# Attention that mixes into token rows, with gate columns, in a fused attention and expert kernel

## The chip, the cores and the metric

One core of a Trainium2 chip. The metric is the device time of one execution in microseconds; runs of one kernel agree within some 0.2%.

## The reference

Two stages run one after the other. The first is a linear attention with a complex decay, for 4 batches, 8 heads, 768 time steps and 48 features a head:

```
mag   = sqrt(a_re^2 + a_im^2);  scale = min(mag, 0.999) / (mag + 1e-6)
S     = (a * scale)[t] * S + k[t] v[t]^T        # S complex, 48 x 48 a head
y[t]  = q[t] . Re(S)
```

Its output, 3072 tokens of 384 features, goes to a mixture of 8 experts. Gate logits are `x @ w_gate`; tokens are assigned greedily by descending logit with a capacity of 384 tokens an expert; each expert computes `relu(x @ w1) @ w2` for its tokens. All data is fp32.

## The kernel before

The 3072 tokens are cut into 24 tiles of 128 (function `unit(i)`); six tiles are one batch. Three tiles form a group (`GC = 3`, 8 groups), on which the elementwise work runs in 1152 columns (`elementwise`). Groups 0 and 7 are cut in two pieces.

*Elementwise.* The decay is turned into running sums of logarithms and angles along time, so that a tile's recurrence becomes matrix products. Stages F1 and F2 square `ar` and `ai` on ScalarE (ACT) into the tiles `s1` and `s2`; F6 adds the two squares. For the groups in `BY_DMA` (groups 1 to 6) F6 is a DMA of GpSimd's queue (POOL) that accumulates `s1` into `s2` (in the trace s<-s); for the others it is an addition on VectorE (DVE). F7 to F10 take logarithm and exponential, S is the scan over time, G3 and G5 scale queries and keys (kq<-kq,s and kq<-kq,zi), N0 scans the angles, T1 and T3 make sines and cosines (tile `CS`). ACT loads one table for exponentials and another for angles in turn; `PLAN` says which stages share a table.

*Per tile.* RK and RQ rotate keys and queries by `CS` into a buffer `f` of 768 columns (f<-kq,CS; `F_BUFS = 4` buffers). Stage K copies `f` into the head-major tile `KQ` with 8 DMAs of SyncE's queue (SP), one a head. Then PE computes the scores (SC, tile sc), DVE masks them (MK, am<-sc,mask), PE transposes the keys (FL, tile kp), ACT copies them out (KC, tile KT), PE multiplies keys by values (ST, tile U) and adds the old state (CA, U<-W,ident), and DVE multiplies by the decay into the next state `W` (WM, W<-U,KQ). The last tile of a batch has no state step, its first one no carry.

*The output of a tile.* MX writes y with features as rows and tokens as columns: the weights are 64 columns of V or W (48 of the head and 16 that belong to the next), the streamed operand is 128 columns of masked scores or queries. A matrix product in fp32 shows as two instructions. ACT copies y out (XC, tile xT). FN turns xT back into token rows by a product with `pick`, a matrix that holds an identity and the gate weights: 96 feature columns and 8 logit columns for each of 4 head pairs (tile xp). ACT copies the features to x and, for the first 18 tiles, the logits to LP (XE); DVE sums the logits over the head pairs (LR, logits<-LP or logits<-xp); a DMA stores x to the token array xd in HBM (XS). The values are loaded in token rows (`load_v`), two groups deep.

*Order.* Every step is recorded with an engine, a cost, a priority and its dependencies (`op`). The planner `in_order` then simulates the engines with these costs, a hop between engines (`HOP`) and a step on one engine (`STEP`), and emits the instructions in the order that it finds; each engine executes its queue in that order. A step's priority is its tile number plus an offset of its kind from the table `OFF`. Where the planner sees PE idle, it puts in filler products (tile hot). The engines' instructions are chained, so nothing reorders them later.

*After attention* the routing finds each expert's tokens, and `experts` gathers token rows from xd, multiplies, and scatters the results. Its order comes from the same planner with its own constants (those whose names begin with M_).

Of the kernel before, what the change touches and what calls it, by code (L numbers as in the profile page):

```python
# [25 lines left out]
GC = 3  # L26
# [30 lines left out]
def constants(nc, con, z, w_gate):  # L57
    v, g = nc.vector, nc.gpsimd

    def t(n, shape, dt=F32):  # L60
        x = con.tile(shape, dt, name=n)
        setattr(z, n, x)
        return x

    jp = t("jp", [128, 128], I32)
    g.iota(jp, pattern=[[1, 128]], base=0, channel_multiplier=-1)
    v.tensor_scalar(t("ident", [128, 128]), jp, 0.0, None, op0=OP.is_equal)
    v.tensor_scalar(t("mask", [128, 128]), jp, 0.0, None, op0=OP.is_ge)
# [12 lines left out]
    t("pid", [128, 1])  # L81
    pick = t("pick", [128, 4, 104])
    v.memset(pick, 0.0)
    for s in range(2):
        r = slice(64 * s, 64 * s + 48)
        v.tensor_copy(pick[r, :, 48 * s:48 * s + 48], z.ident[r, None, r].to_broadcast([48, 4, 48]))
        g.dma_start(pick[r, :, 96:104], w_gate[:, s].rearrange("p d e -> d p e"))
# [157 lines left out]
def attention(nc, real, tc, z, q, k, a_re, a_im, v_tok, xd, later):  # L245
# [8 lines left out]
    LP = con.tile([128, 6, 4, 8], F32, name="LP")  # L254
    v, g = nc.vector, nc.gpsimd
    for i in range(2):
        w = con.tile([96, 400], F32, name=f"W{i}")
        g.memset(w, 0.0)
        W.append(w)
# [5 lines left out]
    for i in range(2):  # L265
        x = con.tile([128, GC, 432], F32, name=f"V{i}")
        g.memset(x[:, :, 384:], 0.0)
        VT.append(x)
# [20 lines left out]
    def dve(n):  # L289
        return n / 960 + 0.1  # L290

    def scan_(n):
        return n * 2.15 / 960 + 0.06

    def dve2(n):
        return n / 1920 + 0.11

    def sca(n, bias=False):
        return n / 1200 + (0.23 if bias else 0.14)
# [46 lines left out]
    def load_v(gi):  # L346
        b, c0, n = GROUPS[gi]
        r = b * S + c0 * 128
# [125 lines left out]
    def unit(i):  # L474
# [3 lines left out]
        v_ = VT[gi % 2]  # L478
# [4 lines left out]
        def KQ():  # L483
            return tiles["KQ", i]

        for hh in range(2):
# [11 lines left out]
            op(("MK", i, hh), "dve", 0.64, at, mask, [("SC", i, hh), ("MX", i - 2)])  # L498
        if cc < 5:
            for hh in range(2):  # L500
# [9 lines left out]
                op(("KC", i, hh), "act", 0.44, at, copy, [("FL", i, hh), ("ST", i - 2), ("ST", i - 3)])  # L510

            def state():
                U = ps.tile([128, 384], F32, name="U")
                mine["U"] = U[:96]
                for h in range(8):
                    for r in HALVES:
                        nc.tensor.matmul(U[r, h * 48:h * 48 + 48], KT[i % 2][:, h * 96 + r.start:h * 96 + r.stop],
                                         v_[:, c, h * 48:h * 48 + 48], start=(h == 0), stop=(h == 7 and not cc), skip_group_check=True)

            def carry():  # L520
                nc.tensor.matmul(mine["U"], z.ident[:96, :96], W[cc % 2][:, :384], start=False, stop=True,
                                 skip_group_check=True)
            op(("ST", i), "pe", 1.33, at - 0.2, state, [("KC", i, 0), ("KC", i, 1), ("lv", gi), ("WM", i - 1), ("WM", i - 2)])
            if cc:
                op(("CA", i), "pe", 0.65, at - 0.1, carry, [("ST", i), ("WM", i - 1), ("WM", i - 2)])
            else:
                made["CA", i] = made["ST", i]

            def gate():
                return KQ()[:, :, 256:257].to_broadcast([96, 8, 48])  # L530

            def nxt():
                return W[(cc + 1) % 2][:, :384].rearrange("p (a b) -> p a b", a=8)
            op(("WM", i), "dve", 0.52, at,
# [3 lines left out]
        def mix():  # L538
            Wc = W[cc % 2]
            y = ps.tile([128, 4, 128], F32, name="y")  # L540
            mine["y"] = y
            for p in range(4):
                for inter in range(2 if cc else 1):
                    for h in (2 * p, 2 * p + 1):
                        o = y[64 * (h % 2):64 * (h % 2) + 64, p]
                        e = slice(h * 48, h * 48 + 64)
                        if inter:
                            nc.tensor.matmul(o, Wc[:, e], KQ()[:, h, 128:256], start=False, stop=True)
                        else:
                            nc.tensor.matmul(o, v_[:, c, e], mine["am", h // 4][:, h % 4], start=True, stop=(cc == 0))  # L550

        def evac():
            xT = wk.tile([128, 4, 128], F32, name="xT")
            mine["xT"] = xT
            nc.scalar.activation(xT, mine["y"], AF.Copy)

        def turn():
            xp = ps.tile([128, 4, 128], F32, name="xp")
            mine["xp"] = xp
            for p in range(4):  # L560
                for r in HALVES:
                    nc.tensor.matmul(xp[r, p, :104], mine["xT"][:112, p, r], z.pick[:112, p], start=True, stop=True)

        def out():
            x = wk.tile([128, 4, 96], F32, name="x")
# [8 lines left out]
        def logits():  # L574
            if i >= MOST:
                v.tensor_reduce(z.lg[:, i], mine["xp"][:, :, 96:104].rearrange("p a e -> p e a"), op=OP.add, axis=AX.X)
# [7 lines left out]
        op(("MX", i), "pe", 1.9 if cc else 1.0, at, mix,  # L584
           [("MK", i, 0), ("MK", i, 1), ("lv", gi), ("XC", i - 1)] + ([("WM", i - 1)] if cc else []))
        op(("XC", i), "act", 0.54, at - 0.1, evac, [("MX", i), ("FN", i - 2)])
        op(("FN", i), "pe", 0.9, at + 0.6, turn, [("XC", i), ("XE", i - 1), ("LR", i - 1)])
        if i == nu - 1:
            op(("LR", i), "dve", 0.45, at, logits, [("FN", i)])
        op(("XE", i), "act", 0.46, at, out, [("FN", i), ("XS", i - 2)] + ([("LR", i)] if i == nu - 1 else []))  # L590
        op(("XS", i), "dma", 0.546, at, store, [("XE", i)])
        if i < nu - 1:
            op(("LR", i), "dve", 0.15 if i % 6 < 5 else 0.45, at, logits, [("FN", i)])
# [4 lines left out]
    for gi in range(G):  # L598
# [10 lines left out]
        if gi + 2 < G:  # L609
            load(("lv", gi + 2), 2.2, elementwise_at + 4, load_v(gi + 2),  # L610
                 [("MX", gi * GC + c) for c in range(GC)] + [("ST", gi * GC + c) for c in range(GC)])
    for n, fn in enumerate(later):
        op(("later", n), "dve", 1.0, NT - 1.0, lambda fn=fn: fn(nc), [("later", n - 1)])
# [45 lines left out]
BY_DMA = [(gi, 0) for gi in range(1, 7)]  # L659
# [4 lines left out]
OFF = {"A1": 7.7532, "F1": -8.0, "F10": -0.2852, "F11": 6.1629, "F2": 1.0958, "F3": 3.1048, "F4": 3.0098, "F5": -8.0, "F6": 8.0, "F7": -6.5322, "F8": 3.2365, "F9": 5.0508, "FL": 2.946, "FL<": -3.9259, "FN": 4.3835, "G1": -0.6071, "G2": 4.4992, "G3": 8.0, "G4": -8.0, "G5": -5.9505, "K": 1.9006, "KC": -0.4768, "LR": -3.8173, "MK": -2.5243, "MX": -4.6482, "N0": 0.976, "N1": -8.0, "N2": -5.5169, "P0": -6.2872, "R0": -7.514, "R1": -4.516, "R2": 3.2639, "R3": 4.827, "R4": -4.8476, "R5": -0.5791, "S": 6.954, "SC": 3.4101, "SC<": -8.0, "ST": 0.3675, "ST<": -0.421, "T1": 7.9956, "T2": 6.9667, "T3": -8.0, "TL": 5.7027, "UA": -3.4084, "UA<": -5.1223, "WM": 0.1274, "XC": 7.799, "XC<": -7.3842, "XE": 4.4086, "XS": 0.7846, "la": -5.6357, "later": -8.0, "li": -5.3368, "lk": -1.3428, "lv": 6.2134, "RK": -2.7051, "RQ": -3.6666, "table": -0.5748, "CA": 3.7656, "BE": -7.9653}  # L664
CHAIN = ("scalar", "vector", "tensor", "gpsimd", "sync")
F_BUFS, KC_BUFS = 4, 5
# [767 lines left out]
def _lay_out(inputs):  # L1434
    import numpy as np

    def feature_major(a):
# [9 lines left out]
        "v": c(inputs["v"].transpose(0, 2, 1, 3)).reshape(N, DM),  # L1447
# [19 lines left out]
```

## Time and profile before

| | us |
|---|---|
| median of 3 timed runs | 517.16 (516.69 to 517.54) |
| the profiled execution | 518.87 |
| its span, first to last instruction | 517.1 |
| PE, DVE, ACT, POOL busy in the span | 433.3, 408.0, 273.5, 93.3 |
| DMA queue of SP: share of 16 engines' span | 27.5% |
| DMA queue of POOL: share | 24.2% |

Engines are PE (TensorE; PEld is its weight load), DVE (VectorE), ACT (ScalarE), POOL (GpSimd) and SP (SyncE, which here only issues DMAs). In a row of instructions, out<-in names the tiles; an "idle" time with an arrow names what ended the wait.

### The profile page before, as it was taken

The numbers are of one execution on the slowest core, as the hardware profiler recorded it, in microseconds if no ns is written. First come the engines' busy times: TensorE is split into PE (matmuls) and PEld (weight loads), VectorE is DVE, ScalarE is ACT, GpSimd is POOL, SyncE is SP. The second block draws the span as 40 slices with busy tenths as digits, with TensorE's granted clock in tenths as the row PEclk, the third lists the DMA queues.
The fourth block names the chain that finished last, engine by engine and source line by source line (L and its number), as shares of the span: only waits on it lengthen the run. The fifth ranks groups of instructions, "written<-read, shape, count | busy, mean of one in ns | idle before, by whom it ended". The sixth has DMA issues, their size and how long they took to land.

```text
span 517.1 us, 10712 instructions
## 1 busy us (share of the span) xinstructions
PE 433.3 (84%) x4138; PEld 377.7 (73%) x4147; DVE 408.0 (79%) x1182; ACT 273.5 (53%) x436; POOL 93.3 (18%) x127
## 2 busy tenths in 40 slices
PE   0008889798989998995699999999999999999992
PEld 0007768585868787895588679888988789999991
DVE  6989879998899999745846699798998998755420
ACT  6996868896878795711012444254424525354410
POOL 3000101010010000000020422425222242530101
PEclk9999999999999999997599999999999999999997
DMA  7866878898888676631260623562160623660101
GB/s 241 252 187 160 232 206 274 222 229 268 236 250 255 189 237 185 190 104 47 67 225 1 225 112 136 185 259 78 36 270 31 260 77 138 253 251 5 43 0 46
DMA packets 47234, 86.11 MB, mean 167 GB/s; under 512 B 5344, under 2 KB 41056, under 8 KB 45136
## 3 DMA queue, kind: packets, MB, share of 16 engines
q1 hardware_dynamic: 39104, 42.56, 27.5%
q0 software_dynamic: 7648, 42.29, 24.2%
q8 instruction: 32, 0.52, 0.4%
q10 hardware_dynamic: 432, 0.59, 0.3%
q14 instruction: 18, 0.15, 0.1%
HBM read 53.49 MB, written 9.44 MB: 122 GB/s over the span
## 4 chain that ended last, share of the span: by engine, by line
PE 32%; DVE 20%; issue 14%; DMA 12%; SPq 11%; ACT 5%; POOL 3%; POOLq 0%; DVEq 0%; ACTq 0%
PE acc L138 21%; SPq L138 11%; DMA KQ<-f 4%; DMA ai<-in_a_im 3%; PE y L138 3%; DVE hl L138 3%; ACT s L138 2%; DVE f L138 2%; PE cnt L138 2%; PE sc L138 2%; DVE p L138 2%; DMA V<-in_v 2%; DMA ar<-in_a_re 2%; DVE zi L138 2%; POOL out L138 2%
## 5 line engine op out<-in xcount | busy, mean ns | idle before, releaser
L138 PE MATMUL sc<-KQ 96*128 96x128 f32 x384 | 50.7, 286 | 41.2 <-DMA KQ<-f 41.2
L138 PEld LDWEIGHTS sc<-KQ 96*128 96x128 f32 x384 | 48.0, 199 | 44.6 <-DMA KQ<-f 42.1
L138 ACT ACTIVATE hh<-acc 128x384 fp32r<-128x384 f32 x56 | 27.5, 491 | 71.1 <-PE acc L138 64.7
L138 PE MATMUL acc<-xh,w1h 128*128 128x384 f32 x168 | 53.5, 350 | 0.9 <-ACT w1h L138 0.7
L138 PE MATMUL acc<-w2h,hl 128*128 128x384 f32 x168 | 54.2, 347 | 0.0
L138 PE MATMUL acc<-w2l,hh 128*128 128x384 f32 x168 | 53.4, 345 | 0.5 <-DVE w2l L138 0.4
L138 PE MATMUL acc<-w2h,hh 128*128 128x384 f32 x168 | 53.1, 344 | 0.0
L138 PE MATMUL acc<-xl,w1h 128*128 128x384 f32 x168 | 52.5, 344 | 0.0
L138 PE MATMUL acc<-xh,w1l 128*128 128x384 f32 x168 | 52.1, 344 | 0.0
L138 POOL DMA_INDIRECT out<-ot,idx x24 | 27.5, 1146 | 95.3 <-ACT ot L138 86.8
L138 DVE TENSOR_TENSOR f<-kq,CS 128x768 f32<-128x768 f32 x48 | 43.5, 950 | 0.4 <-ACT CS L138 0.4
L138 DVE SCALAR_TENSOR_TENSOR hl<-acc,hh 128x384 fp32r<-128x384 f32 x56 | 30.7, 551 | 15.1 <-ACT hh L138 14.3
L138 DVE TENSOR_TENSOR ind<-m,thr 128x768 bf16<-128x768 f32 (+1 forms) x45 | 34.0, 774 | 9.5 <-PE thr L138 8.8
L138 PE MATMUL y<-am,V 128*64 128x128 f32 x384 | 37.4, 283 | 0.9 <-ACT xT L138 0.5
L138 DVE TENSOR_TENSOR am<-sc,mask 128x512 f32<-128x512 f32 x48 | 32.0, 683 | 5.2 <-PE sc L138 5.0
L138 POOL DMA_INDIRECT xg<-xd,idx x24 | 25.9, 1079 | 53.6 <-DVE idx L138 23.9
L138 ACT ACTIVATE ot<-acc 128x384 f32<-128x384 f32 x24 | 11.8, 490 | 40.5 <-PE acc L138 19.8
L138 PEld LDWEIGHTS acc<-xh,w1h 128*128 128x128 f32 x168 | 31.1, 188 | 2.7 <-ACT w1h L138 1.0
L138 PE MATMUL y<-KQ,W 96*64 96x128 f32 x320 | 31.6, 273 | 0.6 <-DVE W L138 0.5
L138 PEld LDWEIGHTS acc<-w2h,hh 128*128 128x128 f32 x168 | 31.1, 188 | 1.1 <-issue 0.6
L138 PEld LDWEIGHTS acc<-w2l,hh 128*128 128x128 f32 x168 | 30.9, 188 | 1.4 <-DVE w2l L138 0.7
L138 PEld LDWEIGHTS acc<-xl,w1h 128*128 128x128 f32 x168 | 31.1, 188 | 0.6 <-DVE xl L138 0.2
(193 smaller groups left out, 1049.6 us busy)
## 6 DMA issues: line engine op xcount, KB each, us to landing
KQ<-f SPq DMA_DIRECT2D x192, 96.4 KB, 2.6
kq<-in_k SPq DMA_DIRECT2D x8, 576.0 KB, 5.6
kq<-in_q SPq DMA_DIRECT2D x8, 576.0 KB, 6.7
V<-in_v SPq DMA_DIRECT2D x8, 576.0 KB, 8.7
xd<-x POOLq DMA_DIRECT2D x21, 192.0 KB
ar<-in_a_re SPq DMA_DIRECT2D x6, 576.0 KB, 4.3
ai<-in_a_im SPq DMA_DIRECT2D x6, 576.0 KB, 8.5
s<-s POOLq DMA_DIRECT2D x6, 576.0 KB
```

Of the source, the lines that this page charges most:

```text
L138: r = f(*a, **k)
```

## The change

- *Output in token rows.* MX now takes the masked scores or the queries as weights (64 tokens a time) and streams V or W: y has tokens as rows and 56 columns a head. XC, FN and the tiles xT and xp go.
- *Gate columns.* A head's values are 48 features and 8 gate columns (`VC = 56`). V is loaded feature-major, and a product with `pick` (VX, tile vx) gives 128 tokens by 8 x 56 columns, which ACT copies to SBUF (VE, tile vt, three buffers). So the state has 56 columns a head, and logits come out of the same y.
- *State in parts of 64.* The state product U keeps its 64-column weights and streams 56 columns; the carry and the decay product go over 448 columns.
- *Dependencies.* The next mix waits for x and the logits of the tile before (they read y); a V buffer is free once VX has read it. The last tile's logits read y.
- *Sums of squares.* `BY_DMA` is empty: F6 of all groups is an addition by DVE.
- *Order.* New planner costs and hops, a new table `OFF`, `F_BUFS` from 4 to 5.

```
-HOP = 0.2
-STEP = 0.06
+VC = D + E
+HOP = 0.13
+STEP = 0.0
...
-            nc.sync.dma_start(VT[gi % 2][:, :n, :384], v_tok[r:r + n * 128].rearrange("(c p) e -> p c e", p=128))
+            nc.sync.dma_start(VT[gi % 2], v_in[b, :, :, t].rearrange("j p t -> p j t"))
...
+        def values():
+            vx = ps.tile([128, 4, 2 * VC], F32, name="vx")
+            mine["vx"] = vx
+            for p in range(4):
+                for n, r in enumerate(HALVES):
+                    t = slice(c * 128 + 64 * n, c * 128 + 64 * n + 64)
+                    nc.tensor.matmul(vx[r, p], VT[gi % 2][:, p, t], z.pick[:, p].rearrange("p a b -> p (a b)"), start=True, stop=True)
+
+        def keep():
+            v_ = st.tile([128, H * VC], F32, name="vt", bufs=VT_BUFS)
+            mine["v"] = v_
+            nc.scalar.activation(v_, mine["vx"].rearrange("p a b -> p (a b)"), AF.Copy)
+        op(("VX", i), "pe", 0.65, at - 1.0, values, [("lv", gi), ("VE", i - 1)])
+        op(("VE", i), "act", 0.52, at - 1.0, keep, [("VX", i), ("MX", i - VT_BUFS), ("ST", i - VT_BUFS)])
...
         def mix():
             Wc = W[cc % 2]
-            y = ps.tile([128, 4, 128], F32, name="y")
+            y = ps.tile([128, H, VC], F32, name="y")
             mine["y"] = y
-            for p in range(4):
+            for h in range(8):
+                o = slice(h * VC, h * VC + VC)
                 for inter in range(2 if cc else 1):
-                    for h in (2 * p, 2 * p + 1):
-                        o = y[64 * (h % 2):64 * (h % 2) + 64, p]
-                        e = slice(h * 48, h * 48 + 64)
+                    for r in HALVES:
                         if inter:
-                            nc.tensor.matmul(o, Wc[:, e], KQ()[:, h, 128:256], start=False, stop=True)
+                            nc.tensor.matmul(y[r, h], KQ()[:, h, 128 + r.start:128 + r.stop], Wc[:, o], start=False, stop=True)
                         else:
-                            nc.tensor.matmul(o, v_[:, c, e], mine["am", h // 4][:, h % 4], start=True, stop=(cc == 0))
-
-        def evac():
...
-        def turn():
...
+                            nc.tensor.matmul(y[r, h], mine["am", h // 4][:, h % 4, r], mine["v"][:, o], start=True, stop=(cc == 0))
...
-            nc.scalar.activation(x, mine["xp"][:, :, :96], AF.Copy)
+            nc.scalar.activation(x, mine["y"][:, :, :D], AF.Copy)
             if i < MOST:
-                nc.scalar.activation(LP[:, i % 6], mine["xp"][:, :, 96:104], AF.Copy)
+                nc.scalar.activation(LP[:, i % 6], mine["y"][:, :, D:], AF.Copy)
...
-        op(("MX", i), "pe", 1.9 if cc else 1.0, at, mix,
-           [("MK", i, 0), ("MK", i, 1), ("lv", gi), ("XC", i - 1)] + ([("WM", i - 1)] if cc else []))
-        op(("XC", i), "act", 0.54, at - 0.1, evac, [("MX", i), ("FN", i - 2)])
-        op(("FN", i), "pe", 0.9, at + 0.6, turn, [("XC", i), ("XE", i - 1), ("LR", i - 1)])
+        op(("MX", i), "pe", 2.05 if cc else 1.0, at, mix,
+           [("MK", i, 0), ("MK", i, 1), ("VE", i), ("XE", i - 1), ("LR", i - 1)] + ([("WM", i - 1)] if cc else []))
...
-BY_DMA = [(gi, 0) for gi in range(1, 7)]
+BY_DMA = []
...
-OFF = {"A1": 7.7532, ...}
+OFF = {'A1': 6.2113, ...}
...
-F_BUFS, KC_BUFS = 4, 5
+F_BUFS, KC_BUFS, VT_BUFS = 5, 5, 3
```

## Rows read from the trace of the kernel before

**Rows 1.** Stages: length, busy us (instructions) of PE, PEld, DVE, ACT, POOL; clock, DMA share, GB/s.

```profile
10.00:40.00 30.00, 0.13 (x1) 0.13 (x1) 26.90 (x57) 28.23 (x32) 1.92 (x3) 1.00 0.75 224
40.00:160.00 120.00, 106.27 (x1326) 86.68 (x1334) 109.44 (x180) 94.23 (x125) 10.06 (x16) 0.99 0.80 230
160.00:210.00 50.00, 46.92 (x658) 39.58 (x656) 48.60 (x95) 38.80 (x61) 3.78 (x7) 1.00 0.74 217
40.00:222.35 182.35, 164.60 (x2157) 136.56 (x2167) 167.85 (x293) 140.17 (x199) 14.39 (x24) 0.99 0.77 222
222.35:238.00 15.65, 14.36 (x214) 12.88 (x211) 4.85 (x13) 3.91 (x9) 0.54 (x1) 1.00 0.32 95
0.00:238.00 238.00, 179.09 (x2367) 149.58 (x2376) 205.10 (x386) 178.49 (x246) 21.87 (x63) 0.99 0.74 214
```

**Rows 2.** Timeline, end of attention: start us, us, engine line operation tiles [idle before <-releaser].

```profile
219.32 0.69 DVE L138 TENSOR_TENSOR am<-sc,mask 128x512 f32<-128x512 f32 x1 [2.10 <-PE sc L138]
219.93 0.95 DVE L138 TENSOR_TENSOR f<-kq,CS 128x768 f32<-128x768 f32 x1
...
221.40 0.95 DVE L138 TENSOR_TENSOR f<-kq,CS 128x768 f32<-128x768 f32 x1
...
234.66 0.39 PE L138 MATMUL y<-KQ,W 96*64 96x128 f32 x4
...
237.56 0.19 DVE L138 TENSOR_REDUCE logits<-xp 128x8 f32<-128x32 f32 x1 [1.04 <-PE xp L138]
```

**Rows 3.** Instruction groups by shape: tiles, count, busy us, mean ns, idle before.

```profile
L138 PE MATMUL hot<-cold 128*128 128x512 bf16 x63 | 15.4, 380 | 0.7 <-PE xp L138 0.5 <-issue 0.2
L138 ACT ACTIVATE xT<-y 128x512 f32<-128x512 f32 x24 | 14.2, 592 | 11.6 <-PE y L138 11.5
L138 ACT ACTIVATE x<-xp 128x384 f32<-128x384 f32 x24 | 11.6, 483 | 8.7 <-PE xp L138 7.1 <-DVE logits L138 1.5
L138 ACT ACTIVATE LP<-xp 128x32 f32<-128x32 f32 x18 | 3.5, 195 | 0.0
```

**Rows 4.** Waits of DVE, 40 to 222.35: total us, times, longest.

```profile
DVE f L138 <- DMA KQ<-f: 6.1, 5, 1.5
DVE am L138 <- PE sc L138: 3.9, 6, 2.1
```

**Rows 5.** DMA issues, stretches 80:92, 175:200 and 105:126: KB each, median us to landing.

```profile
KQ<-f SPq DMA_DIRECT2D x4, 96.4 KB, 4.2
...
KQ<-f SPq DMA_DIRECT2D x31, 96.4 KB, 2.4
...
V<-in_v SPq DMA_DIRECT2D x1, 576.0 KB, 10.8
```

**Rows 6.** Chain of work that ended last: start us, us, what.

```profile
17.88 8.01 DMA s<-s
...
59.31 0.87 DVE f L138
...
105.54 1.27 DVE p L138
```

**Rows 7.** Timeline of DVE at the start, behind the transfer s<-s.

```profile
28.25 0.76 DVE L138 TENSOR_SCALAR zi<-s 128x1152 f32<-128x1152 f32 x1 [1.16 <-ACT s L138]
...
30.86 2.95 DVE L138 TENSOR_TENSOR_SCAN zi<-zi,s 128x128 f32<-128x128 f32 x9 [0.58 <-ACT s L138]
```

**Rows 8.** The chain's PE pieces near the end, then the weight loads of U.

```profile
226.99 1.07 PE U L138 x32
228.06 1.77 PE y L138 x32
229.83 0.82 PE U L138 x2
...
232.43 0.86 PE xp L138 x16
...
220.11 1.01 PEld L138 LDWEIGHTS U<-V,KT 128*64 128x64 f32 x32
```

More of the change, by code (lines that the diff above doesn't have):

```diff
@@ L81, in constants @@
     t("pid", [128, 1])
-    pick = t("pick", [128, 4, 104])
+    pick = t("pick", [96, 4, 2, VC])
     v.memset(pick, 0.0)
     for s in range(2):
-        r = slice(64 * s, 64 * s + 48)
-        v.tensor_copy(pick[r, :, 48 * s:48 * s + 48], z.ident[r, None, r].to_broadcast([48, 4, 48]))
-        g.dma_start(pick[r, :, 96:104], w_gate[:, s].rearrange("p d e -> d p e"))
+        r = slice(48 * s, 48 * s + 48)
+        v.tensor_copy(pick[:, :, s, :48], z.ident[:96, None, r].to_broadcast([96, 4, 48]))
+        g.dma_start(pick[r, :, s, 48:], w_gate[:, s].rearrange("p d e -> d p e"))
     z.lg = t("logits", [128, NT * E + 2])[:, :NT * E].rearrange("p (c e) -> p c e", e=E)
@@ L242, in in_order, with attention @@
     return done
-def attention(nc, real, tc, z, q, k, a_re, a_im, v_tok, xd, later):
+def attention(nc, real, tc, z, q, k, a_re, a_im, v_in, xd, later):
     ctx = ExitStack()
@@ L253, in attention @@
     W, VT = [], []
-    LP = con.tile([128, 6, 4, 8], F32, name="LP")
+    LP = con.tile([128, 6, H, E], F32, name="LP")
     v, g = nc.vector, nc.gpsimd
     for i in range(2):
-        w = con.tile([96, 400], F32, name=f"W{i}")
-        g.memset(w, 0.0)
-        W.append(w)
+        W.append(con.tile([96, H * VC], F32, name=f"W{i}"))
     KT = []
@@ L265, in attention @@
     for i in range(2):
-        x = con.tile([128, GC, 432], F32, name=f"V{i}")
-        g.memset(x[:, :, 384:], 0.0)
-        VT.append(x)
+        VT.append(con.tile([96, 4, T], F32, name=f"V{i}"))
     def table(n):
@@ L289, in dve @@
     def dve(n):
-        return n / 960 + 0.1
+        return n / 960 + 0.067
     def scan_(n):
-        return n * 2.15 / 960 + 0.06
+        return n * 2.05 / 960 + 0.05
     def dve2(n):
-        return n / 1920 + 0.11
+        return n / 1920 + 0.075
     def sca(n, bias=False):
-        return n / 1200 + (0.23 if bias else 0.14)
+        return n / 1200 + (0.195 if bias else 0.1)
     def pool(n):
@@ L497, in unit @@
             op(("SC", i, hh), "pe", 0.9, at - 0.5, scores, KD + [("MK", i - 1, hh)])
-            op(("MK", i, hh), "dve", 0.64, at, mask, [("SC", i, hh), ("MX", i - 2)])
+            op(("MK", i, hh), "dve", 0.6, at, mask, [("SC", i, hh), ("MX", i - 2)])
         if cc < 5:
@@ L509, in unit @@
                 op(("FL", i, hh), "pe", 0.34, at - 0.45, flip, KD + [("KC", i - 1, hh), ("KC", i - 2, hh)])
-                op(("KC", i, hh), "act", 0.44, at, copy, [("FL", i, hh), ("ST", i - 2), ("ST", i - 3)])
+                op(("KC", i, hh), "act", 0.38, at, copy, [("FL", i, hh), ("ST", i - 2), ("ST", i - 3)])
             def state():
-                U = ps.tile([128, 384], F32, name="U")
+                U = ps.tile([128, H * VC], F32, name="U")
                 mine["U"] = U[:96]
                 for h in range(8):
+                    o = slice(h * VC, h * VC + VC)
                     for r in HALVES:
-                        nc.tensor.matmul(U[r, h * 48:h * 48 + 48], KT[i % 2][:, h * 96 + r.start:h * 96 + r.stop],
-                                         v_[:, c, h * 48:h * 48 + 48], start=(h == 0), stop=(h == 7 and not cc), skip_group_check=True)
+                        nc.tensor.matmul(U[r, o], KT[i % 2][:, h * 96 + r.start:h * 96 + r.stop],
+                                         mine["v"][:, o], start=(h == 0), stop=(h == 7 and not cc), skip_group_check=True)
             def carry():
-                nc.tensor.matmul(mine["U"], z.ident[:96, :96], W[cc % 2][:, :384], start=False, stop=True,
+                nc.tensor.matmul(mine["U"], z.ident[:96, :96], W[cc % 2], start=False, stop=True,
                                  skip_group_check=True)
-            op(("ST", i), "pe", 1.33, at - 0.2, state, [("KC", i, 0), ("KC", i, 1), ("lv", gi), ("WM", i - 1), ("WM", i - 2)])
+            op(("ST", i), "pe", 1.0, at - 0.2, state, [("KC", i, 0), ("KC", i, 1), ("VE", i), ("WM", i - 1), ("WM", i - 2)])
             if cc:
-                op(("CA", i), "pe", 0.65, at - 0.1, carry, [("ST", i), ("WM", i - 1), ("WM", i - 2)])
+                op(("CA", i), "pe", 0.76, at - 0.1, carry, [("ST", i), ("WM", i - 1), ("WM", i - 2)])
             else:
@@ L529, in gate @@
             def gate():
[L530 removed]
+                return KQ()[:, :, 256:257].to_broadcast([96, H, VC])
             def nxt():
[L533 to L534 removed]
+                return W[(cc + 1) % 2].rearrange("p (a b) -> p a b", a=8)
+            op(("WM", i), "dve", 0.58, at,
                lambda: v.tensor_tensor(nxt(), mine["U"].rearrange("p (a b) -> p a b", a=8), gate(), op=OP.mult),
@@ L539, in mix @@
             Wc = W[cc % 2]
-            y = ps.tile([128, 4, 128], F32, name="y")
+            y = ps.tile([128, H, VC], F32, name="y")
             mine["y"] = y
-            for p in range(4):
+            for h in range(8):
+                o = slice(h * VC, h * VC + VC)
                 for inter in range(2 if cc else 1):
-                    for h in (2 * p, 2 * p + 1):
-                        o = y[64 * (h % 2):64 * (h % 2) + 64, p]
-                        e = slice(h * 48, h * 48 + 64)
+                    for r in HALVES:
                         if inter:
-                            nc.tensor.matmul(o, Wc[:, e], KQ()[:, h, 128:256], start=False, stop=True)
+                            nc.tensor.matmul(y[r, h], KQ()[:, h, 128 + r.start:128 + r.stop], Wc[:, o], start=False, stop=True)
                         else:
-                            nc.tensor.matmul(o, v_[:, c, e], mine["am", h // 4][:, h % 4], start=True, stop=(cc == 0))
-        def evac():
-            xT = wk.tile([128, 4, 128], F32, name="xT")
-            mine["xT"] = xT
-            nc.scalar.activation(xT, mine["y"], AF.Copy)
-        def turn():
[L558 to L562, printed above, removed]
+                            nc.tensor.matmul(y[r, h], mine["am", h // 4][:, h % 4, r], mine["v"][:, o], start=True, stop=(cc == 0))
         def out():
-            x = wk.tile([128, 4, 96], F32, name="x")
+            x = wk.tile([128, H, D], F32, name="x")
             mine["x"] = x
-            nc.scalar.activation(x, mine["xp"][:, :, :96], AF.Copy)
+            nc.scalar.activation(x, mine["y"][:, :, :D], AF.Copy)
             if i < MOST:
-                nc.scalar.activation(LP[:, i % 6], mine["xp"][:, :, 96:104], AF.Copy)
+                nc.scalar.activation(LP[:, i % 6], mine["y"][:, :, D:], AF.Copy)
         def store():
@@ L583, in logits @@
                     v.tensor_reduce(o[:, 1:2], r, op=OP.min, axis=AX.X)
-        op(("MX", i), "pe", 1.9 if cc else 1.0, at, mix,
-           [("MK", i, 0), ("MK", i, 1), ("lv", gi), ("XC", i - 1)] + ([("WM", i - 1)] if cc else []))
-        op(("XC", i), "act", 0.54, at - 0.1, evac, [("MX", i), ("FN", i - 2)])
-        op(("FN", i), "pe", 0.9, at + 0.6, turn, [("XC", i), ("XE", i - 1), ("LR", i - 1)])
+        op(("MX", i), "pe", 2.05 if cc else 1.0, at, mix,
+           [("MK", i, 0), ("MK", i, 1), ("VE", i), ("XE", i - 1), ("LR", i - 1)] + ([("WM", i - 1)] if cc else []))
         if i == nu - 1:
-            op(("LR", i), "dve", 0.45, at, logits, [("FN", i)])
-        op(("XE", i), "act", 0.46, at, out, [("FN", i), ("XS", i - 2)] + ([("LR", i)] if i == nu - 1 else []))
+            op(("LR", i), "dve", 0.45, at, logits, [("MX", i)])
+        op(("XE", i), "act", 0.56 if i < MOST else 0.46, at, out, [("MX", i), ("XS", i - 2)] + ([("LR", i)] if i == nu - 1 else []))
         op(("XS", i), "dma", 0.546, at, store, [("XE", i)])
         if i < nu - 1:
-            op(("LR", i), "dve", 0.15 if i % 6 < 5 else 0.45, at, logits, [("FN", i)])
+            op(("LR", i), "dve", 0.2 if i >= MOST else 0.8 if i == MOST - 1 else 0.35 if i % 3 == 0 and i else 0.01, at, logits,
+               [("MX", i)] + ([("XE", i)] if i == MOST - 1 else []))
     def load(key, cost, at, fn, deps=()):
@@ L609, in attention @@
         if gi + 2 < G:
-            load(("lv", gi + 2), 2.2, elementwise_at + 4, load_v(gi + 2),
-                 [("MX", gi * GC + c) for c in range(GC)] + [("ST", gi * GC + c) for c in range(GC)])
+            load(("lv", gi + 2), 2.2, elementwise_at + 4, load_v(gi + 2), [("VX", gi * GC + c) for c in range(GC)])
     for n, fn in enumerate(later):
-        op(("later", n), "dve", 1.0, NT - 1.0, lambda fn=fn: fn(nc), [("later", n - 1)])
+        op(("later", n), "dve", 0.1, NT - 1.0, lambda fn=fn: fn(nc), [("later", n - 1)])
     def choices():
```

9 lines of the change are left out of this document (4 added, 5 removed).

## The prediction

> **What bounds the kernel now.** I read the table by stage first [rows 1]. The program has two halves. Attention runs to 238.0 us; routing and experts follow, to the span's end at 517.1. The diff touches no line of these, so I leave the 279 us behind 238 as they are and look for the whole effect ahead of it.
>
> Inside attention no engine is the bound by a wide margin, but VectorE (DVE) comes first: it works 167.85 of the 182.35 us between 40 and 222.35 [rows 1], where 222.35 is the end of the last rotation (the second f row of [rows 2]: 221.40 + 0.95). ScalarE has 140.2 us there. PE shows 164.6, of which 15.4 us are the filler multiplications named hot [rows 3], so 149.2 us of real work and 33 us to spare. So DVE has 14.5 us of idle time before the last rotation, and behind that rotation comes a tail of 15.6 us in which DVE works only 4.85. The waits of DVE [rows 4] say what the idle time is: 6.1 us are waits of f, the rotated tile, for KQ<-f: a rotation may not start until the copy out of an older f buffer has landed. They are five, none over 1.5 us. 3.9 us are masks waiting for scores. The DMA rows [rows 5] say why copies are late at times: beside the accumulating transfer s<-s the median KQ<-f took 4.2 us from issue to landing, in a stretch without one 2.4 us.
>
> **The change part by part.** Every term is taken for its effect on the end of attention, in the profiled execution.
>
> *The sums of squares move from DMA to DVE.* Six additions of 1152 columns come to DVE. A product of the same shape, p<-p,s, takes 1.27 us in a row of DVE instructions (the chain's piece at 105.54) [rows 6]: 6 x 1.27 = 7.6 us. DVE is the fullest engine, so I charge all of it.
>
> *The state carries the gate columns.* The product W<-U grows from 8 x 48 = 384 to 8 x 56 = 448 columns, 20 times. Two back-to-back durations give the slope: 1152 columns 1.27 us, 768 columns 0.87 us (f), so 1.04 ns per column and 64 x 1.04 = 0.067 us; x 20 = 1.3 us. DVE's other work keeps its counts (rotations, scans, masks, logits, which now read y instead of xp). DVE in all: +8.9 us. Lower end +1.3 (the six sums fall wholly into idle time), upper end +8.9.
>
> *The transfers s<-s go.* At the start this is a chain: the transfer for group 1 took 8.01 us [rows 6], and two DVE instructions behind it (zi<-s, then the scan zi<-zi,s) found DVE idle for 1.16 and 0.58 us [rows 7]. The sum by DVE takes 1.27 us in place of 8. I take -1.7 us, these two waits. The bounds are 0 (ScalarE is busy 28.2 of the 30 us from 10 to 40 [rows 1], and the first rotation waits for its sine tables) and -3.1, all of DVE's idle time there. Later the six transfers hid behind other work, so their going saves only what they cost others, next.
>
> *F_BUFS 4 to 5, a free DMA path, a new order.* A fifth f buffer lets the two rotations of one more tile (2 x 0.87 = 1.7 us) start before the oldest copy has landed; no wait of this kind was longer than 1.5 us, so all 6.1 us go. Of the other 8.4 us of DVE's idle time I take a quarter, -2.1 us: the one mask that held DVE for 2.10 us at 219.32, with the last two rotations queued behind it [rows 2], is of that size. Bounds: 0 for both (a new order brings new waits of the same total) and -14.5, all of it.
>
> *PE: mixing into token rows.* Before, a tile with a state needs 32 instructions y of 1.77 us and 16 xp of 0.86 us [rows 8]. Now y takes 64 instructions, each loading 64 columns of weights and streaming 56; the nearest row is U, with 64 weight columns and 48 streamed: 32 in 1.07 us [rows 8], so 64 take 2.14 us, +0.37 us. xp goes, and vx (16 instructions of 112 columns for 104) comes at about the same 0.9 us, but before the mix instead of behind it. The carry grows from 384 to 448 columns: 0.82 x 64 / 384 = 0.14 us at most. Per tile +0.5, x 20 = 10 us against 33 us to spare, so no charge before 222. The cost without that cover is a rival below. vx puts a new wait into PE's queue: it needs V, and all scores and mixes queue behind it. V took up to 10.8 us to land [rows 5]; but its buffer is now free once vx has read it rather than after the mixes and state products, so it can be loaded earlier: nothing, at worst one landing, 10.8.
>
> *ScalarE.* xT of 512 columns (0.592) goes, a copy of 448 columns comes; between that and the 0.483 of 384 columns [rows 3] it takes 0.54. It is a wash, -1 us over 24 tiles off the path. The next mix now waits for x and LP (0.483 + 0.195) where it waited for xT (0.592) [rows 3]: 0.09 us, inside PE's spare time. In the last six tiles the next mix also waits for a logits reduction on DVE; behind a long DVE instruction that is up to 1.3 us each, 0 to 8 us. I take 0 because rotations of those tiles are mostly done by then.
>
> *The tail.* Today the last y starts at 234.66 and ends at 235.05; then come xT on ACT, xp on PE and the logits at 237.56 [rows 2]. Now the logits read y, some 0.15 us behind its end: 237.56 - 235.05 - 0.15 = 2.4 us saved. One xp that stood ahead of the last y goes too, 0.86 us [rows 8]. Against that, two mixes and a carry lie in the tail: 2 x 0.37 + 0.14 = 0.9. Net -2.4 us; bounds 0 and -3.3.
>
> **Sum:** +8.9 - 1.7 - 6.1 - 2.1 - 2.4 = -3.4 us. The profiled execution took 518.87 us with a span of 517.1; so 515.5 us for it. The median of the timed runs is 517.16, 1.7 below that execution, so I forecast 513.8 us.
>
> **The rivals.**
>
> *DVE simply gets longer (slower).* DVE's idle time is not lost buffers but the rhythm of tables, loads and scores, and comes back elsewhere under the new order. For it: from 160 to 210 only 1.4 us of 50 are spare [rows 1], and a wait removed on an in-order engine can show up again at its next instruction. Against it: the f waits have one plain cause and the change adds the buffer. Price: +8.9 - 1.7 - 2.4 = +4.8, 522.0 us. It decides from the point where less than 5 us of the 14.5 us idle go.
>
> *DVE's idle time goes almost wholly.* From 160 to 210 DVE works 48.6 of 50 us, from 40 to 160 109.4 of 120 [rows 1], so the same work can be packed tighter; if the remaining 6.3 us shrink by 5 and the start gives 0.3 more, the time is 508.5 us. Against it: ScalarE and SP serve the same chain.
>
> *It cancels.* Half of the f waits stay (3 us): 517 us.
>
> *PE becomes the bound (slower).* If an instruction of the new mix costs what one of the old does (1.77 / 32 = 0.055 us, weight load and all), the mix takes 64 x 0.055 = 3.5 us, +1.77 a tile, 35 us over 20 tiles plus 3 for the carries: 149.2 + 38 = 187 us of work for 182.35, +5. The tail loses 2 x 1.4 more, so -2.4 becomes +0.4; with the start -1.7 that is +4, 521 us. For it: twice as many weight loads, on an engine that is full in the tail. Against it: the U row, the same weight width at 0.033 us an instruction.
> The Trainium skill speaks for this rival: "TensorE: Matmul & The Clock Gate", section "LDWEIGHTS (loading the stationary operand)", has a weight load take its column count divided by 1.2 in ns, so an estimate of 53 ns for 64 columns and, were loads taken one by one, 64 x 53 = 3.4 us a tile. The trace disagrees on the spacing, if not on the single load: 32 such loads took 1.01 us, 32 ns apart [rows 8], so they overlap, and by this row PE keeps its slack.
>
> **How the numbers follow.** The forecast (511 to 516) gets 0.39, the large gain 0.22, cancelling 0.14, the longer DVE 0.20, PE 0.05. No change means within 0.2%, about 1 us, which is what a measurement of this kernel can tell. Faster is the first two and a sliver of the third: 0.62. Same 0.13. Slower 0.25. The likeliest case's own range is 511 to 516; with the rivals of both signs 506 to 522, which leaves out the far ends of the large gain and of the two slower cases. The unknown costs (late V, late logits, 8 to 11 us) reach past it and have little chance.
>
> **What would show it.** Right: in the profile after, DVE is busy 213 to 215 us up to the end of attention, a little before 236; the waits f<-KQ<-f are below 2 us in all; a mix of 64 instructions takes 2.1 to 2.2 us and U stays at 1.1; KQ<-f lands in 2.4 us or less as a median; the logits of the last tile start within 0.3 us of its last y; the stretch from there to the end is 279 us as before. Wrong: DVE idle over 12 us between 40 us and the last rotation, mixes at 3 us or more, waits of the mix for logits or of vx for V of several us, or an expert stage that differs by more than 1 us.

## The result, and the profile after

The changed kernel takes 513.61 us, the median of 12 runs (511.99 to 520.4), beside 518.87 for the kernel before in 12 runs (516.3 to 524.34). The ratio is 0.9906 with an interval of 0.9877 to 0.9935: faster by about 0.9%. Forecast were 513.8 us and a range of 506 to 522. The runs of one kernel spread by some 1.6%, not by the 0.2% that three runs had suggested at the start. The one execution profiled with the result was a disturbed one (519.89 us), so the rows of after come from a second run of the same kernel, below, whose profiled execution took 513.84 us.

The table by stage answers to [rows 1]. Columns: window and length in us, busy us (instructions) of PE, PEld, DVE, ACT, POOL, then granted clock, DMA share, GB/s. The last rotation now ends at 222.99 (222.35 before).

```profile
0.00:235.50 235.50, 195.64 (x3137) 158.75 (x3152) 216.76 (x392) 178.41 (x246) 16.90 (x53) 1.00 0.72 202
10.00:40.00 30.00, 15.50 (x101) 8.77 (x103) 28.99 (x57) 28.90 (x35) 0.00 (x0) 1.00 0.69 196
40.00:222.99 182.99, 168.21 (x2818) 139.34 (x2829) 177.23 (x297) 140.51 (x198) 12.88 (x21) 1.00 0.75 208
222.99:235.50 12.51, 11.93 (x224) 10.63 (x221) 4.81 (x11) 2.50 (x6) 0.00 (x0) 1.00 0.36 97
235.12:511.80 276.68, 253.28 (x1771) 227.74 (x1771) 203.16 (x799) 95.07 (x191) 69.97 (x64) 0.96 0.35 127
```

DVE worked 167.85 us between 40 and the last rotation and works 177.23 now; its idle time there fell from 14.5 to 5.8 us, and that from 10 to 40 from 3.1 to 1.0. The waits of DVE in this stretch (total us, times, longest) answer to [rows 4], where f<-KQ<-f stood first with 6.1 us:

```profile
DVE am L139 <- PE sc L139: 1.3, 2, 1.1
DVE neg L139 <- ACT p L139: 0.8, 1, 0.8
DVE f L139 <- DMA KQ<-f: 0.7, 3, 0.2
```

The groups of instructions (tiles, shape, count | busy us, mean ns | idle before) give the new work of DVE up to 235.5:

```profile
L139 DVE TENSOR_TENSOR W<-U,KQ 96x448 f32<-96x448 f32 x20 | 12.2, 611 | 1.0 <-PE U L139 1.0
L139 DVE TENSOR_TENSOR s<-s,s 128x1152 f32<-128x1152 f32 x6 | 8.1, 1345 | 0.0
```

The end of attention, first two lines of the timeline and then the chain of work that ended last, answers to [rows 2] and [rows 8]:

```profile
221.16 1.83 DVE L139 TENSOR_TENSOR f<-kq,CS 128x768 f32<-128x768 f32 x2 [0.29 <-ACT CS L139]
...
235.12 0.23 DVE L139 TENSOR_REDUCE logits<-y 128x8 f32<-128x64 f32 x1 [1.54 <-PE y L139]
```

```profile
226.43 0.92 PE vx L139 x16
227.34 0.93 PE U L139 x32
228.27 1.87 PE y L139 x64
230.13 0.92 PE U L139 x2
```

A mix of 64 instructions takes 1.87 us, 29 ns each, beside 1.77 for the 32 of before. The last logits start at 235.12 (237.56 before), 12.1 us behind the last rotation instead of 15.2. So in these two executions attention is 2.44 us shorter: DVE +11.7 us of work up to the last rotation, -11.1 of idle time, -3.1 in the tail, together -2.5.

From the last logits to the end it is 276.7 us, beside 279.5 before. Most of that need not be the change's: a second profiled execution of the kernel before (e8, below) has 277.5 in the same stretch:

```profile
237.08:514.60 277.52, 254.18 (x1771) 228.78 (x1771) 203.09 (x799) 95.01 (x191) 70.94 (x64) 0.95 0.35 127
```

### The profile page after: what moved, and what is told of

It is laid out like the page before. It is cut to its first block, busy times and chain, and to the rows that moved or that the text cites. A ratio compares the mean times of both kernels' runs of the same rounds, so it can differ in the third digit from the quotient of the medians.

```text
span 517.8 us, 12236 instructions
## 1 busy us (share of the span) xinstructions
PE 455.2 (88%) x4908; PEld 390.7 (75%) x4923; DVE 419.9 (81%) x1188; ACT 273.5 (53%) x436; POOL 85.7 (17%) x117
## 4 chain that ended last, share of the span: by engine, by line
DVE 35%; PE 26%; issue 17%; DMA 9%; SPq 5%; POOL 4%; ACT 3%; POOLq 0%; DVEq 0%; ACTq 0%
PE acc L139 16%; DVE neg L139 6%; DVE f L139 5%; DMA KQ<-f 5%; SPq L139 5%; DVE zi L139 4%; DVE am L139 3%; DVE hl L139 3%; DMA xg<-xd,idx 2%; DVE p L139 2%; PE cnt L139 2%; PE y L139 2%; DVE w2l L139 2%; DVE kq L139 2%; POOL out L139 2%
## 5 line engine op out<-in xcount | busy, mean ns | idle before, releaser
L139 PE MATMUL vx<-pick,V 96*64 96x112 f32 x384 | 25.2, 276 | 28.8 <-DMA V<-in_v 25.3
L139 PE MATMUL sc<-KQ 96*128 96x128 f32 x384 | 49.5, 283 | 0.0
L139 PEld LDWEIGHTS vx<-pick,V 96*64 96x64 f32 x384 | 19.9, 144 | 36.4 <-issue 24.9
L139 POOL DMA_DIRECT2D xd<-x x21 | 12.5, 597 | 204.5 <-ACT LP L139 136.1
L139 PE MATMUL y<-vt,am 128*64 128x56 f32 x768 | 44.0, 224 | 2.0 <-DVE am L139 1.4
L139 PEld LDWEIGHTS y<-vt,am 128*64 128x64 f32 x768 | 37.1, 137 | 9.7 <-DVE am L139 7.1
L139 POOL DMA_INDIRECT out<-ot,idx x24 | 26.2, 1093 | 96.6 <-ACT ot L139 88.4
L139 PE MATMUL y<-W,KQ 96*64 96x56 f32 x640 | 38.5, 222 | 0.0
L139 PE MATMUL hot<-cold 128*128 128x512 bf16 x129 | 33.4, 404 | 1.4 <-issue 1.3
```

The costliest lines, as they stand in the source:

```text
L139: r = f(*a, **k)
```

## The experiments

The theory behind the forecast: DVE is the bound; the change charges it in full and gives back more, mainly the f waits by the fifth buffer. The main rivals: the gain is in another part of the change; the old waits only move. Each kernel but e8 was timed in five rounds beside the kernel before; ratios are to that kernel.

**e1, the changed kernel again.**

> The changed kernel once more, for a profile that lies near its median. The prediction's theory (the fuller VectorE is paid for by waits that go): the end of attention near 234 us of the span, VectorE idle between 40 us and the last rotation 6 to 8 us, waits of f for KQ<-f below 1 us, KQ<-f landing in 2.4 us or less, time 512 to 514 us. The rival that VectorE simply gets longer: attention ends at 239 us or later also in this run and the time is 518 us or more.

513.84 us, ratio 0.992 (0.9885 to 0.9955). The result repeats. One figure clearly misses what was expected: the copies KQ<-f are no faster than before. Their DMA issues from 40 to 222 (count, KB each, median us to landing), first before, then e1:

```profile
KQ<-f SPq DMA_DIRECT2D x181, 96.4 KB, 2.6
```

```profile
KQ<-f SPq DMA_DIRECT2D x177, 96.4 KB, 2.7
```

**e2, four f buffers in the changed kernel**, in the same written order.

```
-            return get("f", i, [128, 3, 2, 257], bufs=F_BUFS)
+            return get("f", i, [128, 3, 2, 257], bufs=4)
```

> The changed kernel with four f buffers in place of five, every instruction in the same order on every engine. The prediction's theory: waits of f for KQ<-f come back with 3 to 6 us and the time rises by 3 to 6 us, to 517 to 520 us. The rival that the waits went because the new order spaces rotations and copies otherwise: below 1 us of such waits, time within 1 us of the changed kernel.

539.04 us, ratio 1.0395 (1.0339 to 1.045): 25 us on top of e1, where 3 to 6 were expected. The waits of DVE from 40 to 250:

```profile
DVE f L139 <- DMA KQ<-f: 23.2, 11, 7.1
```

The new order is built on the fifth buffer. This shows what the buffer is worth to that order, not what it gave the kernel before; e5 asks that.

**e3, sums by DMA in the changed kernel** (groups 1 to 6, issued in the same place).

```
-lambda: v.tensor_tensor(G_("s2"), G_("s2"), G_("s1"), op=OP.add)
+lambda: g.dma_start(out=G_("s2"), in_=G_("s1"), accum_op=OP.add)     # gi 1 to 6
```

> The changed kernel with the sums of squares of groups 1 to 6 again by accumulating DMA, all other instructions in the same order. VectorE loses 6 x 1.27 = 7.6 us of work. If the sum by VectorE costs its full duration, as the prediction charged, and its return is only 1.7 us at the start and some of 2 us of copies, this kernel is 3 to 5 us faster, 509 to 511 us. If the transfer's 8 us hold ScalarE's logarithm and what follows in its queue, it is slower: with 8 - 1.3 = 6.7 us for each transfer that is not hidden, 520 us or more if one in five is not.

529.25 us (524.4 to 535.27), ratio 1.0187 (1.0101 to 1.0274): slower than e1 by 15 us as a median and by 11 in its lowest run, although DVE lost about 8 us of work. The waits of ACT up to 245:

```profile
ACT x L139 <- PE y L139: 24.8, 10, 8.5
ACT s L139 <- DMA s<-s: 10.1, 3, 6.2
```

ACT waits for the sums themselves in the second line, and far longer for mixes that PE reaches late. In an order fitted to a sum of a bit over a microsecond, a sum of some 8 us comes late for what follows it; that this is also why the mixes are late is argued, not shown. This kernel can't say whether a transfer costs anything where the order leaves time for it; e6 and e9 do.

**e4, a product of DVE issued twice** (F3, groups 1 to 6, with the same output): +7.6 us of DVE work by the forecast's figure, 8.1 in its trace.

```
+        def f3():
+            for _ in range(2 if 1 <= gi <= 6 else 1):
                 v.scalar_tensor_tensor(G_("p", bufs=2), G_("ar"), TINY, G_("ai"), ...)
```

> The changed kernel with one VectorE instruction of 1152 columns (the product p<-ar,ai) issued twice in groups 1 to 6, same order else: 6 x 1.27 = 7.6 us more of VectorE work and no new dependence. If VectorE is the bound of attention, the time rises by 6 to 8 us, to 520 to 521 us. If its idle time takes part of it up, by 2 to 4 us. If PE has become the bound, by less than 2 us.

523.4 us, ratio 1.009 (1.0052 to 1.0128), 9.6 us above e1. DVE is the bound of the changed kernel's attention: what it gets more, the end gets in full, and a little over.

**e5, five f buffers in the kernel before**, nothing else.

```
-            return get("f", i, [128, 3, 2, 257], bufs=F_BUFS)
+            return get("f", i, [128, 3, 2, 257], bufs=5)
```

> The kernel before with five f buffers in place of four, same order on every engine. The prediction's theory: the 6.1 us of VectorE's waits of f for KQ<-f go and the time falls by 4 to 6 us, to 513 us or so. The rival that a wait taken away under an order made for four buffers comes back at the next instruction of the queue: the f waits go, but other waits of VectorE grow and the time falls by less than 2 us.

521.08 us, ratio 1.0018 (0.9975 to 1.006): no change. Its waits of DVE from 40 to 224.58, the end of its last rotation:

```profile
DVE am L138 <- PE sc L138: 9.6, 14, 1.9
DVE p L138 <- DMA ar<-in_a_re: 3.6, 2, 2.0
DVE W L138 <- PE U L138: 1.8, 3, 0.8
```

The f waits for KQ<-f are gone, all 6.1 us; the masks' wait for scores went from 3.9 us to 9.6, and that of the products p for the load of ar from 1.5 to 3.6. Rotations start up to 1.9 us sooner (141.61 for 143.49), but a copy out takes as long as before (2.7 us as a median from 40 to 222, 2.6 before), and the scores aren't ready when DVE reaches the mask. The buffer alone moved much of the wait to instructions behind it. Not all of the rise is the buffer's: up to 180 us the masks' wait is 5.4 us (1.8 before), and another 3.2 us from 180 to 215, where the kernel before has none, come with a granted clock of 0.78 from 200 to 212 (1.00 before). The gain of 4 to 6 us that was expected lies outside the interval all the same.

**e6, sums by DVE in the kernel before**, at the place in the order where the DMA was issued; four buffers, the old mix and the old order stay.

```
-lambda: g.dma_start(out=G_("s2"), in_=G_("s1"), accum_op=OP.add)
+lambda: v.tensor_tensor(G_("s2"), G_("s2"), G_("s1"), op=OP.add)
```

> The kernel before with all sums of squares on VectorE, issued where the accumulating DMA was issued, same order else. The prediction's terms: +7.6 us of VectorE work, -1.7 at the start, -2 from faster copies: 3 to 5 us slower. The rival that VectorE's idle time of the kernel before takes the sums up: within 1 us of it. The rival that the transfer itself held the pipeline: 2 us faster or more.

515.34 us, ratio 0.9886 (0.9841 to 0.993): as fast as the whole change, within the intervals, where the prediction's terms made it 3 to 5 us slower. By stage, up to the end of its last rotation and behind it, then its waits of DVE in the middle stretch:

```profile
10.00:40.00 30.00, 0.58 (x2) 0.50 (x2) 29.33 (x59) 28.81 (x33) 0.00 (x0) 1.00 0.56 187
40.00:219.70 179.70, 163.67 (x2156) 137.07 (x2165) 171.57 (x296) 138.97 (x198) 10.98 (x20) 0.99 0.72 211
219.70:235.30 15.60, 14.35 (x214) 12.87 (x211) 4.81 (x12) 3.86 (x9) 0.54 (x1) 1.00 0.32 96
```

```profile
DVE am L138 <- PE sc L138: 3.0, 3, 2.1
DVE f L138 <- DMA KQ<-f: 1.4, 2, 0.8
```

DVE has 6.2 us more work up to the last rotation and 8.8 us less idle time. The f waits fell from 6.1 to 1.4 us with four buffers. The tail stays at 15.2 us (219.70 to logits at 234.9). What changed for f is how fast its copies land. The DMA issues of one stretch, 108 to 120 (count, KB each, median us to landing): in both kernels the loads of kq (two), V and ai are under way on SP's queue, and in the kernel before an s<-s as well; first before, then e6:

```profile
KQ<-f SPq DMA_DIRECT2D x7, 96.4 KB, 6.5
s<-s POOLq DMA_DIRECT2D x1, 576.0 KB
V<-in_v SPq DMA_DIRECT2D x1, 576.0 KB, 10.8
```

```profile
KQ<-f SPq DMA_DIRECT2D x6, 96.4 KB, 3.4
V<-in_v SPq DMA_DIRECT2D x1, 576.0 KB, 5.9
```

The other three stretches with an s<-s behind 40 go the same way, two of them with fewer loads issued in e6: 3.1 us before and 2.2 in e6 from 60 to 72, 4.1 and 2.5 from 87 to 97, 5.4 and 2.5 from 138 to 150.

**e7, vx issued twice in the changed kernel**: +21.6 us of PE work by the rows of vx (24 tiles of 0.9 us).

```
+                    for _ in range(2):
                         nc.tensor.matmul(vx[r, p], VT[gi % 2][:, p, t], ...)
```

> The changed kernel with the 16 instructions vx of each tile issued twice, same order: 24 x 0.9 = 21.6 us more of PE work and no new dependence. If PE has slack in attention and VectorE is the bound, as the prediction said, the time rises by 0 to 3 us. If PE has become the bound, by 10 us or more. In between: PE's slack is there but the tail and the waits of VectorE for scores take part of it, 3 to 10 us.

520.13 us, ratio 0.9986 (0.9957 to 1.0014), 6.3 us above e1 by the medians, some 3.4 by the two ratios. At least 15 of the 21.6 us were hidden: PE has slack, but not over every stretch, and it isn't free of price.

**e8, the kernel before in one look.**

> The kernel before in one more profiled execution, to see how far its two halves vary from one execution to the next. If the stretch behind the last logits is 276 to 278 us here, the 2.8 us by which it was shorter in the changed kernel's profile are variation; if it is 279 us or more again, they belong to the change.

516.34 us, span 514.6, last logits at 237.08, f waits of 6.0 us. In these two executions attention of before agrees to half a microsecond; the stretch behind it differs by 2.

**e9, e6 with the traffic put back**: beside each of the six sums a DMA of the same size accumulates one spare tile into another; nothing waits for it.

```
-lambda: v.tensor_tensor(G_("s2"), G_("s2"), G_("s1"), op=OP.add)
+lambda: (v.tensor_tensor(G_("s2"), G_("s2"), G_("s1"), op=OP.add), v.memset(load1[:, 0, 0:1], 0.0),
+         g.dma_start(out=load2, in_=load1, accum_op=OP.add))
```

> The kernel before with the sums on VectorE in the same order, and beside each of the six sums an accumulating DMA of the same size from one spare tile to another, which nothing waits for: the sums no longer wait for a transfer, but the traffic and the place in GpSimd's queue are there as before. If the kernel before lost its time to the transfer's bytes (late copies KQ<-f), the gain of the sums alone (ratio 0.989) goes and the time is that of the kernel before, within 1 us. If it lost it to the wait of logarithm and exponential behind the transfer's 8 us, the gain stays: ratio 0.988 to 0.991, with waits of f for KQ<-f near 6 us again.

521.26 us, ratio 1.0045 (1.0002 to 1.0089): the gain of e6 is gone, and 0.4% more. Its stretch from 10 to 40 and that from 40 to 225.24, its last rotation, the waits of DVE in the latter, then the DMA issues from 138 to 150 and from 108 to 120:

```profile
10.00:40.00 30.00, 0.00 (x0) 0.00 (x0) 29.01 (x60) 28.82 (x34) 1.92 (x3) 1.00 0.77 223
40.00:225.24 185.24, 170.16 (x2165) 141.36 (x2167) 172.95 (x301) 139.82 (x198) 14.41 (x24) 0.96 0.76 218
```

```profile
DVE am L138 <- PE sc L138: 6.1, 5, 2.5
DVE f L138 <- DMA KQ<-f: 3.1, 5, 1.0
```

```profile
KQ<-f SPq DMA_DIRECT2D x7, 96.4 KB, 4.5
...
load<-load POOLq DMA_DIRECT2D x1, 576.0 KB
```

```profile
load<-load POOLq DMA_DIRECT2D x1, 576.0 KB
...
KQ<-f SPq DMA_DIRECT2D x4, 96.4 KB, 2.8
```

So with such transfers beside them, the sums on DVE gain nothing, though nothing waits for the transfers. How the transfers cost it is shown only in part. The copies are late in two of the four stretches (4.5 us from 138 to 150, 3.5 from 87 to 97) and not in the other two (2.8 from 108 to 120, 2.3 from 60 to 72), and the f waits come back by half (3.1 us, 6.1 before). Filling the spare tiles adds 2.9 us of DVE at the start, and the first rotations are 0.7 us later than in e6 for it; that much of the loss isn't traffic. Of the 5.5 us by which the last rotation ends later than in e6, another 2.6 arise between two rotations (94.44 and 118.19 here, 92.30 and 113.44 there); the granted clock is 0.66 from 100 to 110, where e6 has 1.00 from 100 to 120, and no such transfer is issued between 89.70 and 114.73. Whether the traffic made PE idle and so lowered the clock, or it fell by itself, isn't shown. Nor does e9 separate the bytes on the DMA engines from the place in POOL's queue.

The wait for the sum had its part too: from 10 to 40 DVE is idle for 1.0 us here and 0.7 in e6, where the kernel before has 3.1, so at the start it was the wait and not the traffic that cost DVE some 2 us of idle time.

**e10, the old mix with all the rest of the change**: the kernel before with `BY_DMA` empty, five buffers, the new costs and the new `OFF` (its own offsets kept for steps that only it has).

```
-F_BUFS, KC_BUFS = 4, 5
+F_BUFS, KC_BUFS = 5, 5
```

> The kernel before with its old mix, but with the rest of the change: sums on VectorE, five f buffers, the new planner costs and the new table of offsets (the two steps that the change drops keep their old offsets). If the gain is the sums and the order, ratio 0.985 to 0.992 to the kernel before, as for the sums alone or better. If the new order is worth something with the new mix only, slower than the sums alone: ratio 1.00 or more.

545.31 us, ratio 1.0527 (1.0454 to 1.0601). The stages up to its last rotation and behind it:

```profile
40.00:214.20 174.20, 160.37 (x1744) 122.35 (x1744) 163.31 (x269) 131.53 (x176) 8.66 (x15) 0.96 0.65 191
214.20:266.20 52.00, 50.71 (x757) 43.47 (x756) 16.64 (x35) 13.45 (x29) 3.25 (x6) 1.00 0.43 123
```

The rotations run ahead and leave PE a tail of 52 us. The offsets belong to the structure that they were made for, so this says nothing about the mix: inconclusive.

**e11, the new mix with the old offsets**: the changed kernel with the `OFF` of before for all steps that both have.

```
-OFF = {'A1': 6.2113, 'BE': 11.824, ...}
+OFF = {'VE': 2.3168, 'VE<': -9.0672, 'VX': 9.0599, 'VX<': -2.5563, 'A1': 7.7532, 'F1': -8.0, ...}
```

> The changed kernel with the offsets of the kernel before for all steps that both have (the two new steps keep their own). If the order is a large part of the change, slower by 5 us or more than the changed kernel, over 518 us; if the new mix and the sums carry it whatever the order, within 2 us of 513.8.

521.85 us, ratio 1.0046 (1.0008 to 1.0083), 8 us above e1. Without its order the changed kernel isn't faster than the one before.

**e12, no filler products in the changed kernel.**

```
-FILL, FILL_REST = 0.25, 0.6
+FILL, FILL_REST = 1e9, 0.6
```

> The changed kernel without the 129 filler products on PE, order else the same. If PE's slack is the limit (e7: 21.6 us more PE work cost 6 us), taking 32 us of filler away gives 1 to 4 us, unless the clock falls: then stretches of attention show a granted clock below 1.0 and the time rises by 2 to 8 us.

518.4 us, ratio 0.9995 (0.9951 to 1.0039), 4.6 above e1. Two stretches, from e1's kernel and then from e12 (the eighth figure is the granted clock):

```profile
100.00:130.00 30.00, 27.63 (x438) 21.92 (x441) 29.75 (x53) 27.18 (x33) 1.64 (x2) 1.00 0.82 236
160.00:180.00 20.00, 17.87 (x289) 13.88 (x287) 19.57 (x37) 16.41 (x24) 1.14 (x2) 1.00 0.78 215
```

```profile
100.00:130.00 30.00, 26.36 (x348) 22.27 (x350) 28.29 (x48) 26.06 (x33) 1.62 (x3) 0.77 0.81 235
160.00:180.00 20.00, 17.07 (x223) 14.37 (x223) 18.89 (x35) 14.82 (x20) 0.54 (x1) 0.66 0.83 231
```

With fewer instructions PE is busy nearly as long, because it spends part of the stretch at the lower of its two levels (1.2 instead of 2.4 GHz).

## Why the prediction was right, and which step of it was not

The time came out within 0.2 us, and part of that is luck. The sum said -3.4 us, taken from a median of 517.16 in 3 runs; the medians of 12 runs differ by 5.3, from 518.87. In attention, where the whole effect was forecast, the profiled executions differ by 2.4. A base that was 1.7 us too low and a difference that was 1.9 too small cancelled. The sum's parts, against the profiled executions:

- *DVE's new work*: forecast +8.9 us, measured +11.7 up to the last rotation. The six sums were 8.1 for 7.6 (1345 ns each, not 1270) and W 1.2 for 1.3. Another 1.1 are the six logits sums, now over 192 columns, one set for each of 8 heads, instead of 96 for 4 head pairs (483 ns for 301); I had counted these as unchanged. The other 1.3 us aren't accounted for by groups of instructions: the durations of all groups up to there grow by 10.6 together, and DVE's work behind the last rotation is the same as before (4.81 for 4.85). The charge in full was right (e4).
- *The start*: forecast -1.7 us, measured -2.1 (idle time from 10 to 40, 3.1 to 1.0).
- *DVE's idle time behind 40*: forecast -6.1 for the f waits and -2.1 for the rest, together -8.2; measured -8.7 (14.5 to 5.8), the f waits themselves 6.1 to 0.7. **The size was right and the price of the buffer was not.** The failed step is "A fifth f buffer lets the two rotations of one more tile ... start before the oldest copy has landed; ... so all 6.1 us go", with the sentence ahead of it that the later transfers "hid behind other work". In the old order the buffer alone gives nothing, since other instructions wait instead (e5, ratio 1.0018). The sums' move alone, with four buffers, takes 8.8 us of DVE's idle time, of which 2.4 at the start (e6, ratio 0.9886), and traffic of the same size brings the time back (e9, by a path that is open in part). The 4.2 beside 2.4 us of [rows 5] was the clue, if a rough one: the first stretch has four loads beside the copies as well, the second only one. I booked it as the reason why copies are late and then priced the buffer as the cure; a late copy holds up the scores too, not just the buffer. In the changed kernel the buffer does keep the f waits away, since its copies are no faster (2.7 us, 2.6 before) and four buffers bring 23.2 us of them (e2), but under an order that was written for five.
- *The tail*: forecast -2.4 us, measured -3.1 (15.2 to 12.1). The logits read y as expected, 0.03 us behind its end in the chain's records.
- *PE*: 64 instructions were to take 2.14 us and take 1.87; the slack carried them, and of 21.6 us more some 15 were hidden (e7). The rival in which PE becomes the bound is excluded by 29 ns an instruction where it needed 55. The 53 ns a load are an estimate from the Trainium skill ("TensorE: Matmul & The Clock Gate", section "LDWEIGHTS (loading the stationary operand)"), 64 columns divided by 1.2. No row of this trace shows 53: the record of one such load for y lasts 138 ns as a median, and in a row of them it is 29 ns from one to the next. The prediction left open whether the single load agrees; it doesn't.
- *Order*: I gave it a quarter of the remaining idle time. e11 shows 8 us between two orders of the same work, so it decides whether the change gains anything.
- *The signs*: most that were named for a right reading came. Those that did not: DVE is busy 216.8 us up to the end of attention (213 to 215 forecast), a mix takes 1.87 us (2.1 to 2.2), KQ<-f lands in 2.7 us as a median (2.4 or less), and the stretch behind attention is 2.8 us shorter, which was named as a sign of being wrong from 1 us on. By e8 2.0 of these 2.8 come and go between executions of one kernel; the other 0.8 can't be told from that.

Put together: by the measurements the sums' move to DVE is worth the whole gain (e6: 0.9886, the change: 0.9906). The rest of the change - the mix into token rows, the gate columns, the fifth buffer and the new order - nets about nothing beside it, under the order that it came with (e2 and e3 show that its parts lean on each other, so the ratios don't add up part by part): its tail is 3.1 us shorter, and its last rotation ends 3.3 us later than e6's (222.99 for 219.70), with 5.5 us more work on DVE up to there.

The rival "DVE simply gets longer" was right about the mechanism, a wait that reappears at the next instruction, for the buffer (e5), and wrong about the sum.

What stays open: the timed medians differ by 5 us, the profiled executions by 2.4 in attention and by 2.5 (e8 and e1) as a whole. The 12 runs of the kernel before lie between 516.3 and 524.34, and its two profiled executions (518.87 and 516.34) at their median and below it. What lengthens the others isn't shown; moments at the lower clock, as in e9 and e12, would fit, but that is only argued. Which of bytes and queue place makes the accumulating transfer dear, and how much of e9's loss is the lower clock, wasn't separated either. And what the new mix is worth under an order of its own but with the sums on DMA wasn't tried.

## What to carry to other kernels

Work moved to a free DMA queue isn't free when critical copies are under way beside it: look at what the other queue's transfers take from issue to landing beside it and without it, in stretches with the same other loads, and price that before pricing buffers. A wait removed on an engine that keeps its order can come back at an instruction behind it, as in e5; ask which later instruction needs the same event. An order that was fitted to one structure is part of that structure: single edits tested under it (a buffer less, a slower sum) cost far more than they are worth by themselves, so test each part in the kernel before as well.

## What was not expected of the hardware

- With six accumulating transfers of 576 KB between SBUF tiles beside it, for which nothing waits, the 1.1% that the sums on DVE gave is gone (e6 0.9886, e9 1.0045), a little of it by the setting up and some of it in a stretch at a lower clock. From 108 to 120, beside one of them and four loads, a 96 KB copy of another queue took 6.5 us in the kernel before, and 3.4 beside the loads alone (e6); in e9 it took 2.8 there, so it isn't so each time. The median of all these copies over attention hardly shows it (2.6 before, 2.5 in e6); the stretches do.
- Filler products that compute nothing, 31.9 us of PE time, are worth 4.6 us: without them the granted clock is 0.77 from 100 to 130 and 0.66 from 160 to 180, where it was 1.00 in both.
